# Second token layer of chunk pairs 0-1 and 3-4 as seven block products from batch 2 on

## The chip, the cores and the metric

One core of a Trainium2 chip runs the whole program. The metric is device time in microseconds (us), the median over several runs. The four runs of the kernel before agree within 0.1% (594.19 to 594.73 us); each run also reports the mean clock that TensorE was granted, as a share of full speed.

In this kernel TensorE does the matrix products into PSUM banks, ScalarE and VectorE move results out of these banks (an eviction) and add them up, and GpSimd does adds on SBUF, where the operands lie, and issues part of the transfers. In the views of the profile PE is TensorE, PEld its weight loads, DVE is VectorE, ACT ScalarE, POOL GpSimd and SP the queue of SyncE; `L913` is line 913 of the kernel, and `osb<-px` says that tile `osb` is written from `px`.

A wait is told here in one of two ways. The views count the idle time of TensorE after the recorded end of a product, and leave out what is under 0.15 us. That end is modelled: in the kernel before, a product of 512 columns is recorded with 0.379 us while the next starts after 0.215. So from start to start a wait is some 0.16 us longer than in the view; where a number below is counted so, the text says it.

## The reference, cut to what matters

```python
# x: (8, 3008, 256)
X = real(fft(fft(x, axis=1), axis=2))              # Fourier mixing
xt = X.transpose(0, 2, 1)
h  = maximum(xt @ w_tok1, 0) @ w_tok2              # token layers, 3008 -> 256 -> 3008
u  = X + h.transpose(0, 2, 1)
out = u + maximum(u @ w_ch1, 0) @ w_ch2            # channel layers, 256 -> 1536 -> 256
```

There are eight batches. The change concerns `@ w_tok2`, the second token layer, and the addition of X to it.

## The kernel before: the parts that matter

A batch's 3008 tokens are worked on in six chunks of 512 columns (`CW`). For each batch a generator yields the pieces of the Fourier and token layers; the main loop deals them out over 24 steps per batch, of some 2.9 us each, between the products of the channel layers of the batch before. The second token layer makes a chunk's two halves by two products each and one VectorE add:

```python
for c in range(NCH):
    if c in (1, 2):
        third(c)                     # 8 small products, ScalarE copy qs, two VectorE adds: yt
        yield
    ut = perb.tile([P, 2, CW], FP16, tag="ut", name="ut", bufs=4)
    # ... cuts: the last, shorter chunk; the first chunk of batch 0
    for h in range(2):
        pu = ps_f("pu")
        for th in range(2):
            nc.tensor.matmul(pu[:, 0:n], lhsT=uu[:, th, int(minus), h, :],
                             rhs=w2_cols(b, c)[:, th],
                             start=(th == 0), stop=(th == 1))
        # ... y: the part of yt that belongs to this half
        nc.vector.tensor_tensor(out=ut[:, h, 0:n]..., in0=pu[:, 0:n]..., in1=y..., op=AT.add)
    yield
```

The fold adds the mirrored half of the next input to the straight one. `xp` and `xm` come by transfers that GpSimd issues; the first add that reads `xm` waits for them:

```python
for s, (t0, t1) in enumerate(((13, 17), (9, 13), (5, 9), (1, 5))):
    # ...
    tt(out=xp[:, t, 1:D], in0=xp[:, t, 1:D], in1=xm[0:KR, rv, D - 1:0:-1], op=add)
    yield
    # ... then two or three adds into eo; yield between them
fold_plan = [[0] * 8 + [1, 2, 0, 0] * 4 for _ in range(BB)]     # pieces of it per step
```

The channel layers already use a seven-product scheme: VectorE makes `block_sums` of the activations `c1`, TensorE multiplies them into the banks `px` and `py`, and VectorE takes these banks out by `residual` into `osb`. The main loop, cut:

```python
for s in range(4):
    sub = 4 * c + s
    mm1(b, c, c1, range(3 * s, 3 * s + 3))    # first channel layer: pc -> c (ScalarE)
    # ... block_sums (VectorE), at once or after mm2, by s
    take(own, ...); take(nxt, ...)            # pieces of this batch and of the next
    mm2(*prev, s, pbox)                       # second channel layer: px, py -> osb
    take(nxt, ...)
    # ...
    take(folds, fold_plan[b][sub])            # fold of the batch after next
    if b and sub == 22 and b + 3 < BB:
        x_tiles[b + 3] = load_x(b + 3)        # GpSimd issues the loads of xp and xm
```

## Time and profile before

| | before |
|---|---|
| time, median of 4 runs | 594.2 us (594.19 to 594.73) |
| TensorE busy, matmuls | 580.4 us (98%), 6397 |
| VectorE busy | 458.7 us (77%) |
| ScalarE busy | 437.7 us (74%) |
| GpSimd busy | 152.7 us (26%) |

The prediction below shows the lines of the page, of the chain and of the waits. One more view is wanted for the comparison. I cut the trace at the first matmul of the first channel layer of each batch; these are batches 1, 2 and 3 before. The columns are: stretch in us, its length, then busy us and number of instructions of PE, weight loads, DVE, ACT and POOL, then the granted clock, the share of the DMA engines and GB/s.

```profile
100.52:170.22 69.70, 69.70 (x775) 50.30 (x774) 59.29 (x138) 52.55 (x122) 18.33 (x31) 1.00 0.50 93
170.22:240.89 70.67, 70.67 (x805) 51.45 (x804) 56.53 (x129) 52.88 (x122) 17.81 (x28) 1.00 0.47 91
240.89:310.53 69.64, 69.64 (x776) 50.28 (x775) 55.29 (x129) 52.53 (x122) 16.62 (x28) 1.00 0.48 91
```

TensorE's busy time equals the length of each batch. Odd and even batches differ by 1 us because of the chunk that two batches share, and the later batches repeat these two lengths.

### The profile page before, as it was taken

How to read it: one execution, taken by the hardware profiler on the slowest of the kernel's cores; microseconds unless marked ns; L12 is line 12 of the kernel's file. 1: busy time of each engine (PE TensorE's matmuls, PEld its weight loads, DVE VectorE, ACT ScalarE, POOL GpSimd, SP SyncE). 2: the span in 40 equal slices, each digit the busy share in tenths (PEclk: the TensorE clock that was granted, in tenths of full speed). 3: DMA queues.
4: the chain of work that ended last, by engine and by line, in shares of the span. 5: the costliest groups of instructions: out<-in, count | busy, mean ns of one | idle time of the engine just before them, and what ended most of it. 6: DMA issues, size and time to landing. Idle time of an engine off the chain costs nothing.

```text
span 592.4 us, 15959 instructions
## 1 busy us (share of the span) xinstructions
PE 580.4 (98%) x6397; PEld 419.8 (71%) x6397; DVE 458.7 (77%) x1075; ACT 437.7 (74%) x994; POOL 152.7 (26%) x251
## 2 busy tenths in 40 slices
PE   5999999999999999999999999999999999999997
PEld 4846777767776777676777667767777777866676
DVE  8868689878896887769797787868888677676573
ACT  7775887887778777777767776777777867766772
POOL 7530421412151211421134111421211121112131
PEclk9999999999999999999999999999999999999999
DMA  9996851863367242844329432492233335333424
GB/s 151 211 187 126 139 101 46 150 122 54 66 122 139 55 88 56 157 71 98 64 49 170 98 65 55 90 172 54 56 76 63 78 55 97 48 72 72 82 58 105
DMA packets 86683, 56.55 MB, mean 95 GB/s; under 512 B 54945, under 2 KB 83553, under 8 KB 85857
## 3 DMA queue, kind: packets, MB, share of 16 engines
q1 hardware_dynamic: 77984, 37.77, 33.6%
q0 software_dynamic: 8320, 17.49, 17.2%
q8 instruction: 50, 0.82, 0.6%
q10 hardware_dynamic: 304, 0.26, 0.2%
q14 instruction: 25, 0.20, 0.1%
HBM read 34.98 MB, written 24.64 MB: 101 GB/s over the span
## 4 chain that ended last, share of the span: by engine, by line
PE 96%; DVE 2%; ACT 1%; issue 0%; POOL 0%; DVEq 0%; POOLq 0%
PE pc L773 41%; PE px L817 25%; PE py L817 10%; PE pu L730 7%; PE pt L613 4%; PE po L888 2%; PE pz L518 2%; PE pq L645 1%; PE py L645 1%; PE py L836 1%; PE pw L596 1%; PE pw L597 1%; PE pw L560 0%; ACT z L307 0%; PE ph L430 0%; PE ph L432 0%
## 5 line engine op out<-in xcount | busy, mean ns | idle before, releaser
L776 ACT ACTIVATE c<-pc 128x512 f16<-128x512 f32 (+1 forms) x574 | 297.9, 595 | 31.3 <-PE pc L773 16.3
L799 POOL TENSOR_TENSOR osb<-osb,rt 128x256 f32<-128x256 f32 (+1 forms) x92 | 84.5, 919 | 373.3 <-DVE osb L799 366.1
L817 PEld LDWEIGHTS <-c 128*128 128x128 f16 x2112 | 128.1, 98 | 24.9
L773 PE MATMUL pc<-ut,wc1p 128*128 128x512 f16 x576 | 140.0, 379 | 0.5 <-DVE ut L305 0.5
L773 PE MATMUL pc<-ut,wc1m 128*128 128x512 f16 (+1 forms) x576 | 134.9, 370 | 0.0
L822 ACT ACTIVATE m<-px 128x256 f32<-128x256 f32 (+1 forms) x138 | 51.8, 375 | 75.4 <-PE px L817 46.0
L817 PEld LDWEIGHTS <-sb 128*128 128x128 f16 x1584 | 94.6, 98 | 10.4
L738 DVE TENSOR_TENSOR ut<-pu,yt 128x512 f16<-128x512 f32 (+1 forms) x94 | 63.3, 674 | 40.6 <-PE pu L730 40.3
L773 PEld LDWEIGHTS <-wc1p 128*128 128x128 f16 x576 | 52.0, 97 | 49.2 <-DMA wc1p<-in_moe_w_ch_dram,ixc 0.8
L773 PEld LDWEIGHTS <-wc1m 128*128 128x128 f16 x576 | 52.9, 98 | 45.0
L817 PE MATMUL px<-wst,c 128*128 128x128 f16 x1056 | 74.0, 219 | 0.0
L817 PE MATMUL px<-wc,c 128*128 128x128 f16 x1056 | 66.5, 219 | 0.0
L799 DVE TENSOR_TENSOR osb<-py,m 128x256 f32<-128x256 f32 (+1 forms) x92 | 37.5, 407 | 26.5 <-ACT m L822 26.2
L790 DVE TENSOR_TENSOR sb<-sb,c 128x768 f16<-128x768 f16 (+1 forms) x92 | 54.2, 589 | 3.2
L730 PE MATMUL pu<-w2p,uu 128*128 128x512 f16 (+1 forms) x184 | 54.7, 379 | 0.0
L790 DVE TENSOR_TENSOR sb<-c 128x768 f16<-128x768 f16 (+1 forms) x92 | 50.6, 550 | 0.0
L790 DVE TENSOR_TENSOR c<-c 128x768 f16<-128x768 f16 (+1 forms) x92 | 50.5, 548 | 0.0
L790 DVE TENSOR_TENSOR sb<-c,sb 128x768 f16<-128x768 f16 (+1 forms) x92 | 50.4, 548 | 0.0
L307 ACT ACTIVATE z<-pz 128x480 f16<-128x480 f32 (+1 forms) x60 | 39.0, 666 | 5.4 <-PE pz L527 3.0
L599 DVE SCALAR_TENSOR_TENSOR w<-alt,pw 128x131 f16<-128x131 f16 x84 | 29.2, 351 | 16.5 <-ACT w L307 16.0
L652 DVE TENSOR_TENSOR yt<-py,qs 128x512 f16<-128x512 f32 x48 | 30.9, 685 | 10.5 <-ACT qs L648 10.2
L817 PE MATMUL py<-wst,sb 128*128 128x128 f16 x528 | 37.1, 219 | 0.0
(201 smaller groups left out, 648.1 us busy)
## 6 DMA issues: line engine op xcount, KB each, us to landing
out_dram<-osb SPq DMA_DIRECT2D x83, 256.0 KB, 3.8
xp<-in_x_dram POOLq DMA_DIRECT2D x16, 272.0 KB, 5.3
out_dram<-osb SPq DMA_DIRECT2D x11, 192.0 KB, 3.1
xp<-in_x_dram POOLq DMA_DIRECT2D x16, 127.5 KB, 5.8
rt<-ut SPq DMA_TRANSPOSE x96, 3.8
w2s<-in_moe_w_tok_dram POOLq DMA_DIRECT2D x1, 1504.0 KB, 14.8
w1p<-in_moe_w_tok_dram POOLq DMA_DIRECT2D x4, 192.0 KB, 7.9
wc<-in_moe_w_ch_dram POOLq DMA_DIRECT2D x1, 768.0 KB, 15.2
```

Of the source, the lines that this page charges most:

```text
L307: nc.scalar.activation(out=out_, in_=in_, func=AFT.Copy)
L599: nc.vector.scalar_tensor_tensor(out=w[:, g, 0:131], in0=alt[:], scalar=pw[:, 131:132], in1=pw[:, 0:131], op0=AT.mult, op1=AT.add)
L613: nc.tensor.matmul(pt[:, o:o + n], lhsT=hw[:, g, th * P:th * P + P], rhs=w[:, g, f:f + n], start=(g == 0), stop=(g == NG - 1))
L652: nc.vector.tensor_tensor(out=yt[:, h, CW * c:CW * c + CW], in0=py[:], in1=qs[:], op=op)
L730: nc.tensor.matmul(pu[:, 0:n], lhsT=uu[:, th, int(minus), h, :], rhs=w2_cols(b, c)[:, th], start=(th == 0), stop=(th == 1))
L738: nc.vector.tensor_tensor(out=ut[:, h, 0:n].rearrange("p (a b) -> p a b", b=64), in0=pu[:, 0:n].rearrange("p (b a) -> p a b", b=64), in1=y ...
L773: nc.tensor.matmul(pc[:, 0:n], lhsT=wc[:, h, ct * P:(ct + 1) * P], rhs=ut[:, h, 0:n], start=(h == 0), stop=(h == 1))
L776: nc.scalar.activation(out=c1[:, ct, 0:n], in_=pc[:, 0:n], func=AFT.Relu)
L790: nc.vector.tensor_tensor(out=o, in0=x, in1=y, op=op)
L799: eng.tensor_tensor(out=o, in0=x, in1=y, op=AT.add)
L817: nc.tensor.matmul(o[:, t], lhsT=a(k)[:, f:f + P], rhs=w(k), start=(first and t == 0 and k == 0), stop=(k == HC - 1), skip_group_check=True)
L822: nc.scalar.activation(out=m[:, i, t1], in_=pa[:, 0], func=AFT.Copy)
```

## The change

Its intent is one product fewer in each 2x2 block of (two halves of the feature rows) x (two chunks), by sums of blocks: the weight sums are made once by GpSimd in batch 1, the sums of the activations for every batch by VectorE. The 7 products need 7 VectorE adds out of PSUM in place of 4, so the schedule of all pieces was laid out anew. The diff, cut to its core:

```diff
+    def w2_sums():                                  # once, in batch 1
+        for i, c in enumerate(PAIRS):               # PAIRS = (0, 3)
+            ...
+            for o, x, y in ((t1, b12, b11), (t2, b22, t1), (t3, b22, b12), (t4, b21, t2)):
+                pl.tensor_tensor(out=o, in0=x, in1=y, op=AT.subtract)
+                yield
@@ fold: mirror adds by themselves; from batch 4 on all four come first
+        if b >= 4:
+            for s, (t, rv) in enumerate(parts):
+                mirror(s, t, rv)
+                yield
@@ second token layer, from batch 2 on, chunks 0-1 and 3-4
+            mm(pa, uu[:, 0, m, 0, :], wa[:, 0], True)
+            plus(t0, pa, add_y(0, c), "v")
+            yield
+            mm(px, uu[:, 1, m, 0, :], wa[:, 1], True)
+            plus(into(ua, 0), px, t0)
+            yield
+            mm(pb, usum[:, 0, m, :], wsum[:, i, 0, :], True)
+            mm(pa, usum[:, 1, m, :], wsum[:, i, 1, :])      # adds to what is in pa
+            plus(t1, pa, add_y(0, c + 1), "v")
+            yield
+            ...                                             # pa, pa, pb again
@@ main loop
-    plan = [...] + [[1] * 14 + [2, 1] * 4 + [1, 1]] * (BB - 1)
+    plan = [...]                                    # pieces before and after mm2, by hand
+    sums_plan = [0, 1, 1, 2, 0, 0, 1, 1, 1, 0, 1, 0, 0, 0, 0, 0, 0, 0, 0, 0, 0, 0, 0, 0]
-    fold_plan = [[0] * 8 + [1, 2, 0, 0] * 4 for _ in range(BB)]
+    fold_plan = [[0, 1, 0, 0, 1, 0, 0, 0, 2, 1, 0, 0, 3, 0, 0, 0, 0, 2, 0, 0, 2, 0, 0, 0] for _ in range(BB)]
```

In the new `plan`, eight small products (`third`) and four second-layer products of chunk 2 are also done one batch earlier than before, so batch 1 has more to do and batch 7 less.

## The prediction

The forecast's sum for VectorE came to 31.7 us: the 36 adds of 0.686 us (24.7 us) and the activation sums. It came to 5.3 us in a middle batch with both pairs (60 to 63.6 of some 69.7 us, 86 to 91%) and to 3.2 us for the new pair in batch 1. The trace after shows 0.28 to 0.29 us for an activation sum, 6.9 us for the 24.

> **What bounds the kernel now.** I read the busy shares first, then the chain that ended last, then its pieces in order of time, then the waits of TensorE, then busy time by batch. The page:
>
> ```profile
> PE 580.4 (98%) x6397; PEld 419.8 (71%) x6397; DVE 458.7 (77%) x1075; ACT 437.7 (74%) x994; POOL 152.7 (26%) x251
> PE 96%; DVE 2%; ACT 1%; issue 0%; POOL 0%; DVEq 0%; POOLq 0%
> ```
>
> TensorE is busy 98% and the chain that sets the end is 96% TensorE. Busy alone would not settle it, since the recorded ends of matmuls are modelled. The chain's pieces between 229 and 238 us (start, length, what) do:
>
> ```profile
> 229.65 1.14 PE pc L773 x6
> 230.78 0.43 PE pu L730 x2
> 231.22 1.34 PE px L817 x24
> 232.56 0.43 PE pu L730 x2
> 232.99 1.13 PE pc L773 x6
> 234.12 0.67 PE py L817 x12
> 234.79 0.67 PE px L817 x12
> ```
>
> Each piece starts where the one before ends: 230.78 + 0.43 = 231.21, 231.22 + 1.34 = 232.56. There is no hole, and a second-layer product (the `pu` rows, 512 columns) occupies the chain for 0.43 / 2 = 0.215 us, not for the 0.379 us that its own row gives as duration. The waits of TensorE (engine, line waited for: us, times, longest) over the whole span:
>
> ```profile
> PE filler L294 <- DVE altu L325: 5.9, 1, 5.9
> PE pz L518 <- ACT tt L287: 0.6, 1, 0.6
> PE pc L773 <- DVE ut L305: 0.5, 1, 0.5
> ```
>
> Asked for the time after 40 us alone, this view lists no wait of TensorE. Busy time in two middle batches (stretch: us, PE, weight load, DVE, ACT, POOL):
>
> ```profile
> 110.30:181.10 70.80, 70.80 (x802) 51.30 (x801) 58.25 (x131) 53.13 (x124) 21.05 (x33) 1.00 0.58 106
> 181.10:250.60 69.50, 69.50 (x782) 50.38 (x779) 54.68 (x129) 51.83 (x122) 17.16 (x27) 1.00 0.46 89
> ```
>
> So a batch lasts as long as its matmuls need, at clock 1.00, and the other engines have room: VectorE 54.7 to 58.3 of some 70 us, GpSimd 17 to 21. Only less TensorE work can shorten it; other engines matter once they make TensorE wait. The rows for pricing (busy, mean ns of one, idle before it):
>
> ```profile
> L730 PE MATMUL pu<-w2p,uu 128*128 128x512 f16 x152 | 45.2, 379 | 0.0
> L738 DVE TENSOR_TENSOR ut<-pu,yt 128x512 f16<-128x512 f32 x78 | 53.4, 686 | 35.8 <-PE pu L730 35.6
> L790 DVE TENSOR_TENSOR sb<-c x92: 344/548/1523, 48.9 to 575.0; 128x768 f16<-128x768 f16 x84, 128x384 f16<-128x384 f16 x8
> L703 DVE COPY ut<-tail x4: 184/1184/1186, 135.4 to 554.2; 128x128 f16<-128x128 f16 x4
> ```
>
> The adds behind the second layer spend 35.8 us waiting for TensorE: VectorE is usually ahead.
>
> [...]
>
> **The change part by part.**
>
> TensorE: for chunk pairs 0-1 and 3-4 the 2x2 block product (two halves of the feature rows, two chunks) takes 7 products in place of 8. From batch 2 on that is 6 batches x 2 pairs x 1 = 12 matmuls of 512 columns fewer; the built program confirms it, with 24 rows fewer on TensorE (12 loads, 12 matmuls). All else on TensorE stays in kind and number. 12 x 0.215 = 2.6 us off the path, 0.43 us per batch. The loads lay under matmuls and count nothing. The columns are now contiguous for the summed blocks, which I price at nothing[...].
>
> VectorE: each pair had 4 adds from PSUM and now has 7 (three keep a running partial in SBUF, four finish a chunk half): 12 x 3 = 36 more x 0.686 = 24.7 us. The activation sums are 4 per batch of 128x256 in 16 bit. [...] Together 31.7 us: busy 458.7 becomes about 490, 83% of the span. [...] All of it lies beside TensorE as long as VectorE keeps up.
>
> GpSimd: 8 weight sums of 128x512, once, in batch 1. Its 128x512 residual add takes 1.17 us in the timeline, so I estimate 8 x 1.17 = 9.4 us: 21 becomes 30 of 70.8 us. [...] batch 1 has 70.8 - 58.3 = 12.5 us of VectorE slack and takes only the new pair 0-1[...].
>
> ScalarE: nothing added or removed. The order of `py` and `pq` is exchanged so that the bank which ScalarE reads is filled first; no cost.
>
> What moves: the interleaving of the pieces is laid out anew, and fold work goes earlier. The order of instructions shows the new dependences. The bank `pa` is written four times per pair with an add reading it in between, where each chunk half had its own bank before. Mostly a step of some 2.9 us (24 to a batch) lies between two writes. In the pair 0-1 from batch 2 on, the third and fourth write share a step with 24 small matmuls between them, 1.34 us. The need is 0.379 (first product's latency) + 0.686 (the add) = 1.07 us; from start to start there is 0.215 + 1.34 = 1.56 us. About 0.5 us is left, if VectorE is free at once.
>
> Sum: -2.6 us of matmuls, + new stalls. I choose 0.1 us per batch for six batches (a late VectorE now and then) and 0.1 us for GpSimd in batch 1: +0.7. 594.2 - 2.6 + 0.7 = 592.3 us, a gain of 0.3%.
>
> **The rivals.**
>
> 1. VectorE takes the matmul's place: at near 90% in a batch and strictly in order, it reaches the adds from `pa` late, and TensorE waits at the fourth write and at the block sums of the channel layer. For it: waits already make 12 to 15 us of idle VectorE time per batch, so useful room is less than the share suggests; the margin is only 0.5 us at one place. Against: most of these waits are for TensorE's own products, and the tight place comes once per batch. One stall of 0.4 us per pair would be 12 x 0.4 = 4.8 us: 594.2 - 2.6 + 4.8 = 596.4 us.
>
> 2. GpSimd holds VectorE up in batch 1. For it: the copy of `tail` took 1184 ns in place of 184. Against: it is one batch, there is slack. At worst some 2 us of stalls: about 593.6 us.
>
> 3. Nothing waits, and the re-laid schedule also clears what little TensorE loses in the middle: 591.6 us. Much below that isn't possible, for the matmuls left are the same and start and end of the program are as before.
>
> 4. The saved time is hidden anyway, because the end is set by the last batch's output. Against: the last batch also saves, its chain is TensorE to the end, and the tail after it is unchanged. It would give 594.2 us.
>
> **Range and chances.** The gain is bounded by 2.6 us; I give the full gain without new stalls a quarter, a gain of 1 to 2.4 us half, rival 1 or 2 in strength a quarter. With 0.5 us for the spread of runs (594.19 to 594.73 before), 8 in 10 lie between 591.2 and 594.6. Faster by over 2% would need 11.9 us, more than four times the removed work: 0.01. Slower by over 2% would need a stall of 14.5 us, 1.2 us in each of the 12 pairs: 0.02. The rest, 0.97, is within 2%.
>
> **What would show each step.** Right: 6385 matmuls, the chain still 96% TensorE without holes, batches of about 70.4 and 69.1 us, VectorE near 490 us busy, ScalarE within 1 us of before, GpSimd near 162, no TensorE wait after 40 us. New waits of TensorE for the VectorE rows that read `pa`, or for `sb` and `c`, would show rival 1; long block sums in batch 1 beside GpSimd's weight sums, rival 2. The prediction is wrong if the batches do not get shorter by about 0.4 us each, or if products on summed blocks run at another rate than 0.215 us.

## The result, and the profile after

The changed kernel takes 602.92 us (601.81 to 605.44, four runs) against 594.22. All outputs are right. A ratio here is the mean time of one kernel's runs over that of the other's in the same rounds, so it is not quite the ratio of the medians: 1.0147, 95% interval 1.0121 to 1.0173. It is within 2%, but slower, 8.7 us where 1.9 us of gain were predicted, and outside the range.

The page after, with the clock in fortieths of the span and the chain that ended last:

```profile
PE 582.8 (97%) x6385; PEld 419.6 (70%) x6385; DVE 487.3 (81%) x1135; ACT 438.8 (73%) x994; POOL 167.0 (28%) x259
...
PEclk9999999989999999999999999999999999999999
...
PE 14%; DVE 0%; issue 0%
```

The 12 matmuls are gone and the busy times are close to the predicted ones. But one slice of the clock has an 8, and the chain can be followed back only over the last 14% of the span: it broke at 516.8 us, behind a wait in batch 6, and says nothing of what came before. Shares and chain would have told little; the cut by batches tells more. Batches 1, 2 and 3 after:

```profile
101.74:178.05 76.31, 73.32 (x786) 51.75 (x785) 68.35 (x149) 53.03 (x123) 28.88 (x38) 0.98 0.43 83
178.05:251.61 73.56, 70.85 (x803) 51.33 (x802) 59.32 (x138) 53.06 (x122) 21.04 (x31) 1.00 0.52 96
251.61:321.78 70.17, 69.72 (x774) 50.18 (x772) 59.05 (x138) 52.74 (x122) 17.17 (x28) 1.00 0.47 90
```

Batch 1 grew from 69.70 to 76.31 us. Its 11 more matmuls are the 12 that moved there (8 of 128 columns, 4 of 512) less one of the first pair of batch 2; by start-to-start times of 0.056 and 0.215 us that is 8 x 0.056 + 3 x 0.215 = 1.1 us. The other 5.5 us are waits and a lowered clock. Batch 2 has two matmuls fewer (803 for 805) and is 2.9 us longer. Batches 3 to 6 are 1.5 us longer together, though each lost 0.43 us of products. Batch 7 is shorter, mostly by what moved out of it. The waits of TensorE after the first 38 us (line waited for: us in all, times, longest), of which the kernel before had none after 40 us:

```profile
PE px L931 <- DVE osb L913: 3.2, 6, 1.9
PE py L931 <- DVE osb L913: 2.3, 1, 2.3
PE px L931 <- DVE c L904: 0.4, 1, 0.4
PE pc L887 <- ACT c L890: 0.4, 2, 0.2
PE pa L751 <- DVE tc L760: 0.3, 1, 0.3
```

Of 6.8 us in the view (a sixth line, of 0.2 us, is cut) 5.5 are for `osb`, the eviction of the channel layers' banks by VectorE: not for the adds of the new product. Only 0.3 us is a wait for a read of `pa`. Counted from start to start, and with the slower clock of which more below, TensorE lost 5.7 us in batch 1, 3.4 in batch 2 and 3.5 in batches 3 to 6. Two waits of some 2 us stand out.

**The wait in batch 1.** VectorE, GpSimd and TensorE around 117 us, from the timeline (start, length, what, idle before and who ended it):

```profile
116.57 0.63 DVE L904 TENSOR_TENSOR sb<-c 128x768 f16<-128x768 f16 x1
117.24 3.22 DVE L904 TENSOR_TENSOR sb<-sb,c 128x768 f16<-128x768 f16 x1
120.38 0.41 DVE L913 TENSOR_TENSOR osb<-px,m 128x256 f32<-128x256 f32 x1
```

```profile
116.72 1.01 POOL L913 TENSOR_TENSOR osb<-osb,rt 128x256 f32<-128x256 f32 x1
117.70 1.19 POOL L469 TENSOR_TENSOR w2s<-w2p 128x512 f16<-128x512 f16 x1
118.85 1.19 POOL L469 TENSOR_TENSOR w2s<-w2p,w2s 128x512 f16<-128x512 f16 x1
```

```profile
120.84 0.33 PE L931 MATMUL px<-wst,sb 128*128 128x128 f16 x3 [1.95 <-DVE osb L913]
```

An add of two SBUF operands that takes 0.56 us at the median took 3.22. It ends 0.4 us after the third of three GpSimd instructions that followed one another without a gap (116.72 to 120.04 us; a small copy of 0.52 us comes next): it seems to have got no turn between them, which is my reading of these times. The eviction behind it came late, and TensorE waited 1.95 us. What followed is in the granted clock, the third number from the right in these stretches of the same kernel:

```profile
118.00:120.80 2.80, 0.90 (x14) 0.71 (x12) 2.80 (x3) 1.17 (x3) 2.51 (x3) 1.00 1.02 173
120.80:122.00 1.20, 1.16 (x23) 1.15 (x23) 1.20 (x2) 0.29 (x2) 1.13 (x2) 1.00 0.97 167
122.00:125.60 3.60, 3.60 (x17) 1.68 (x14) 0.59 (x2) 2.70 (x6) 1.25 (x1) 0.55 1.21 212
125.60:130.00 4.40, 4.40 (x50) 3.07 (x48) 3.64 (x9) 3.24 (x8) 0.14 (x1) 0.98 0.00 0
```

From 122.00 to 125.60 us TensorE ran at 0.55 of its clock in the mean, a loss of 0.45 x 3.6 = 1.6 us more. TensorE counts as fully busy in it, so no view of waits shows this loss.

**The wait in batch 2.**

```profile
190.19 0.23 DVE L483 TENSOR_TENSOR xp<-xp,xm 94x16 f16<-94x16 f16 x1 [6.40 <-DMA xm<-in_x_dram,ix]
190.30 0.68 DVE L484 TENSOR_TENSOR xp<-xp,xm 94x1020 f16<-94x1020 f16 x1
190.90 0.41 DVE L913 TENSOR_TENSOR osb<-py,m 128x256 f32<-128x256 f32 x1
```

VectorE stood idle for 6.4 us until a load of the input had landed. The new fold plan has the first mirror add in step 1 of the batch (counted from 0), where it was in step 8; the load is still issued at the change of batch, which is at 178.05 us: GpSimd issues `xp` from 176.81 us and `xm` at 179.23 and 180.51. The eviction of `py` was in the queue behind the fold, and TensorE waited 2.34 us for it.

So there are four suspects: the sums on GpSimd, the early fold, the lowered clock, and small waits in the later batches. A rival to all of them is that seven products cost TensorE as much as eight.

### The profile page after: what moved, and what is told of

The parts are those of the page before. It is cut to its first block, busy times and chain, and to the rows that moved or that the text cites. A ratio compares the mean times of both kernels' runs of the same rounds, so it can differ in the third digit from the quotient of the medians.

```text
span 603.6 us, 15998 instructions
## 1 busy us (share of the span) xinstructions
PE 582.8 (97%) x6385; PEld 419.6 (70%) x6385; DVE 487.3 (81%) x1135; ACT 438.8 (73%) x994; POOL 167.0 (28%) x259
## 5 line engine op out<-in xcount | busy, mean ns | idle before, releaser
L913 POOL TENSOR_TENSOR osb<-osb,rt 128x256 f32<-128x256 f32 (+1 forms) x92 | 85.9, 934 | 381.9 <-DVE osb L913 369.5
L913 DVE TENSOR_TENSOR osb<-py,m 128x256 f32<-128x256 f32 (+1 forms) x92 | 37.4, 407 | 34.2 <-ACT m L936 33.8
L904 DVE TENSOR_TENSOR sb<-c 128x768 f16<-128x768 f16 (+1 forms) x92 | 56.0, 608 | 0.0
L904 DVE TENSOR_TENSOR sb<-c,sb 128x768 f16<-128x768 f16 (+1 forms) x92 | 51.9, 564 | 0.0
L904 DVE TENSOR_TENSOR c<-c 128x768 f16<-128x768 f16 (+1 forms) x92 | 50.5, 548 | 0.0
L931 PE MATMUL px<-wst,sb 128*128 128x128 f16 x528 | 37.0, 219 | 3.2 <-DVE osb L913 3.2
L931 PE MATMUL py<-wc,sb 128*128 128x128 f16 x528 | 37.0, 219 | 2.3 <-DVE osb L913 2.3
L314 ACT ACTIVATE z<-pz 128x480 f16<-128x480 f32 (+1 forms) x60 | 37.2, 726 | 2.6 <-PE pz L561 1.7
L852 DVE TENSOR_TENSOR ut<-pu,yt 128x512 f16<-128x512 f32 (+1 forms) x46 | 29.9, 658 | 8.8 <-PE pu L849 8.6
```

The lines of the kernel that those rows point to most:

```text
L314: nc.scalar.activation(out=out_, in_=in_, func=AFT.Copy)
L852: nc.vector.tensor_tensor(out=ut[:, h, 0:n].rearrange("p (a b) -> p a b", b=64), in0=pu[:, 0:n].rearrange("p (b a) -> p a b", b=64), in1=a ...
L904: nc.vector.tensor_tensor(out=o, in0=x, in1=y, op=op)
L913: eng.tensor_tensor(out=o, in0=x, in1=y, op=AT.add)
L931: nc.tensor.matmul(o[:, t], lhsT=a(k)[:, f:f + P], rhs=w(k), start=(first and t == 0 and k == 0), stop=(k == HC - 1), skip_group_check=True)
```

## The experiments

### Each suspect alone, put into the kernel before

Only the eight weight sums, which nothing reads:

```diff
+    sums_plan = [0, 1, 1, 2, 0, 0, 1, 1, 1, 0, 1] + [0] * 13
+    w2_parts = w2_sums()
...
+                if b == 1:
+                    take(w2_parts, sums_plan[sub])
```

Theory A is the hold read above, 3.22 us for an add of 0.56.

> The kernel before plus nothing but the eight weight sums on GpSimd in batch 1, in the steps where the changed kernel has them; their results are not used. Theory A ([...]TensorE waits over 2 us at one place in batch 1 and then runs some 3.5 us at about half clock): the time rises by 2 to 5 us over the kernel before, all of it in batch 1, with one block sum of VectorE over 2.5 us long. Rival (the sums are harmless, batch 1 of the changed kernel is longer because its new interleaving overloads VectorE): within 0.5 us of before.

Measured: 596.12 us, ratio 1.0032 (1.0016 to 1.0049). Batch 1 is 71.56 us in place of 69.70, and TensorE has two waits that were not there:

```profile
PE py L832 <- DVE osb L814: 0.7, 1, 0.7
PE px L832 <- DVE c L805: 0.7, 1, 0.7
```

The clock stayed full. The sums cost 1.9 us by themselves, a little less than expected, in a batch in which VectorE is less loaded than in the changed kernel (59 us busy in the kernel before, 68 in the changed one). The expected long block sum is there: `c<-c` at 117.78 us took 3.40 us (the 92 of this kind take 54.6 us in all, 50.5 in the kernel before), beside four GpSimd instructions in a row (117.66 to 120.77), two of them weight sums, and ended 0.4 us after the last, as in the changed kernel. The expected wait of over 2 us is not: behind this sum stood another sum, and TensorE lost 0.7 us. So here, with 3.40 us of hold for 0.7 us of wait, it was not the length of the hold alone that counted, but what stood behind it.

Only the new fold and its plan:

```diff
-    fold_plan = [[0] * 8 + [1, 2, 0, 0] * 4 for _ in range(BB)]
+    fold_plan = [[0, 1, 0, 0, 1, 0, 0, 0, 2, 1, 0, 0, 3, 0, 0, 0, 0, 2, 0, 0, 2, 0, 0, 0] for _ in range(BB)]
```

> The kernel before with nothing but the changed kernel's fold order and fold plan, whose first mirror add stands in step 1 of a batch in place of step 9. Theory B (the first mirror add waits at the head of VectorE's queue for the load of x of that batch, which was issued only three steps earlier): VectorE waits 4 to 8 us for the landing of xm in batch 2, TensorE loses about 2.5 us there, and the time rises by 2 to 3.5 us over before; later batches lose under 0.5 us each. Rival (batch 2's loss comes from batch 1's delay or from the block products): no wait of VectorE for xm over 1 us, time within 0.7 us of before.

Measured: 595.81 us, ratio 1.0027 (1.0010 to 1.0043). Batch 2 is 72.35 us in place of 70.67, with one wait:

```profile
PE py L828 <- DVE osb L810: 1.4, 1, 1.4
```

VectorE stood idle for 3.73 us before the first mirror add of batch 2. Both suspects are real, and each was smaller here than expected. In the changed kernel they are larger. That the same batches also hold the new adds there would explain it; this is argued and not shown. The runs with parts taken out, below, show that the two suspects also act on each other.

### Each suspect taken out of the changed kernel

The sums on VectorE in place of GpSimd:

```diff
-                pl.tensor_tensor(out=o, in0=x, in1=y, op=AT.subtract)
+                nc.vector.tensor_tensor(out=o, in0=x, in1=y, op=AT.subtract)
```

> The changed kernel with the eight weight sums on VectorE in the same steps. Theory A: no VectorE instruction in batch 1 is longer than 1.5 us, no stretch of lowered clock after 40 us; the time falls by 3 to 5.5 us below the changed kernel's (602.9), to 597.5 to 600. Rival (VectorE's load itself makes batch 1 long): VectorE has 4 us more to do there, and the time stays or rises above 603.

Measured: 599.43 us (598.40 to 599.65), ratio 1.0089. Batch 1 fell from 76.31 to 72.17 us and no stretch of lowered clock is left. A sum takes 0.42 us on VectorE; on GpSimd it took 1.19 to 1.51. Giving VectorE, the fuller engine, 3.3 us more work made the kernel 3.5 us faster, as expected: what the sums cost on GpSimd was the hold that they had on VectorE, up to the 3.22 us of one add. The fold stood where it was, yet TensorE's wait in batch 2 fell from 2.34 to 0.64 us and that batch to 71.94 us.

The sums spread, one at most in a step:

```diff
-    sums_plan = [0, 1, 1, 2, 0, 0, 1, 1, 1, 0, 1, 0, 0, 0, 0, 0, 0, 0, 0, 0, 0, 0, 0, 0]
+    sums_plan = [0, 0, 0, 0, 0, 1, 1, 0, 0, 1, 1, 0, 0, 1, 1, 0, 0, 0, 1, 0, 0, 0, 1, 0]
```

> The changed kernel with the eight weight sums still on GpSimd but spread: at most one to a step, in steps 5, 6, 9, 10, 13, 14, 18 and 22 of batch 1, away from GpSimd's residual adds and from the load of x. Theory A (back-to-back GpSimd instructions lock VectorE out): no VectorE instruction in batch 1 over 1.8 us, no TensorE stall over 1 us there, no lowered clock; time 598 to 600 (changed kernel 602.9, sums on VectorE 599.4). Rival (any GpSimd work of this size costs the same wherever it stands): above 601.5.

Measured: 601.49 us, ratio 1.0128; the four runs are 599.17 and 600.08 at clocks 0.999 and 1.0, 602.90 and 603.01 at 0.997 and 0.996. The two runs at full clock are what was expected, the median is not. Batch 1 took 73.42 us in the profile. Spreading shortens the worst wait of batch 1, from 2.1 us to 1.0 (start to start), but several remain. Batch 2 fell too, from 73.56 to 71.44 us, though nothing in it was changed. In the profiled run, a fast one, nothing waited longer than that; what lowered the clock in the other two runs was not seen.

The first two mirror adds of batch 2 in steps 5 and 6:

```diff
+    fold_plan[2] = [0, 0, 0, 0, 0, 1, 1, 0, 2, 1, 0, 0, 3, 0, 0, 0, 0, 2, 0, 0, 2, 0, 0, 0]
```

> The changed kernel with the first two mirror adds of batch 2 moved from steps 1 and 4 to steps 5 and 6, all else the same. Theory B: the wait of VectorE for xm in batch 2 shrinks from 6.4 us to under 1, TensorE's stall of 2.5 us at that place goes, and the time falls by 2 to 3 us, to 600 to 601. Rival (VectorE's total load in batch 2 sets its length): under 0.7 us.

Measured: 601.81 us, ratio 1.0132. Batch 2 fell from 73.56 to 71.45 us, so beside the bunched sums the early fold was worth 2.1 us of it. The four runs fall apart again: 599.86 and 600.60 at clock 1.0, which is what was expected, 603.34 and 603.03 at 0.996. The profile fell on a run at full clock: it has the same wait of 1.9 us in batch 1, and no lowered clock after it. So the wait does not always bring the lowered clock with it, and the runs with a lower mean clock are some 2.9 us longer.

Both at once:

> The changed kernel with the sums spread and the first mirror adds of batch 2 moved to steps 5 and 6. If theories A and B are separate terms their gains add: 596.8 to 598.5. Rival (one hides the other): no better than the better of the two alone, about 599.

Measured: 598.81 us (598.63 to 599.44), ratio 1.0077. That is 0.3 us above the range in which the two gains simply add, and close to the 599 of the rival. The runs no longer fall apart. The batches say how far the two are one term: batches 1 and 2 together took 149.87 us in the changed kernel, 5.0 less with the sums spread, 3.8 less with the fold late, and only 5.5 less with both. Once the sums are spread, moving the fold takes batch 2 from 71.44 to 70.99 us, 0.45 and not 2.1. One reason can be read: from the second issue of `xm` to the add that waits for it there were 9.7 us in the changed kernel and 7.5 with the sums spread. Why the load took longer is not shown. With the two large waits gone, 4.6 us above the kernel before are left.

### The small waits

I moved `third` behind the channel product of its step, one of the writes of `pa` to another place, and one `z` piece to a neighbouring step, and made the first mirror adds late in all batches:

```diff
-    plan += [list(zip([0, 0, 1, 0, 0, 0, 0, 0, 1, 0, 0, 1, 0, 2, 0, 0, 1, 2, 1, 0, 1, 0, 0, 0],
-                      [2, 1, 2, 2, 0, 1, 0, 1, 2, 1, 1, 2, 2, 0, 0, 2, 0, 0, 0, 0, 1, 1, 2, 1]))] * (BB - 2)
+    plan += [list(zip([0, 0, 0, 0, 0, 0, 0, 0, 1, 0, 0, 1, 0, 2, 0, 0, 0, 2, 1, 0, 1, 0, 0, 0],
+                      [2, 2, 2, 2, 0, 1, 0, 1, 2, 1, 1, 2, 2, 0, 0, 2, 1, 0, 0, 0, 1, 1, 2, 1]))] * (BB - 2)
```

(and the same in batch 1's lists)

> As x6_both, and three pieces moved within the interleaving: the middle third of the first-layer products of the token inverse (pq, py) behind the channel product of its step in place of before it, one write of pa in batch 1 behind that product as well, one z piece out of the step that held three; late first mirror adds for all batches. Theory C (the repeating stalls of 0.4 us at px and 0.36 or 0.18 us at pc and px in batches 2 to 6 come from VectorE's and ScalarE's queues at two crowded steps, not from the number of instructions): these stalls go, each of batches 3 to 6 gets shorter than the same batch of the kernel before by 0.3 to 0.45 us, time 593 to 595.5. Rival (VectorE is simply too full with 31 us more): the stalls move elsewhere, time stays at 597 or so.

Measured: 596.88 us (596.79 to 597.50), ratio 1.0045 (1.0029 to 1.0062). A wait of 0.41 us (start to start) for `osb`, which every batch from 2 to 6 had behind the two adds of `third`, is gone. The time is above the expected 595.5 all the same: batch 1 is still 73.27 us, and TensorE still loses 0.2 to 0.8 us in each of batches 2 to 6. By the time alone the rival, a VectorE that is simply too full, did as well (597 or so); the later plans, with the same work in another order, speak against it.

### Is the saved product worth anything?

To the kernel of the last run I added the eighth product back, by issuing the second product of each pair twice. It writes the same values again:

```diff
-            mm(px, uu[:, 1, m, 0, :], wa[:, 1], True)
+            for _ in range(2):
+                mm(px, uu[:, 1, m, 0, :], wa[:, 1], True)
```

> As x7_relaid, with the second product of each pair issued twice (the second overwrites the first with the same values): 8 products per pair in place of 7, 12 matmuls of 512 columns more, nothing else. If TensorE's chain sets the time, it takes 12 x 0.215 = 2.6 us more than x7_relaid (2.2 to 2.8). Rival (VectorE or the waits set the time and matmuls are hidden): under 1 us more.

Measured: 598.60 us against 596.88. In the traces each step with the doubled product is 0.21 to 0.22 us longer, and the last product of the first channel layer comes 2.41 us later. One of the twelve fell into a wait and cost nothing. The rival is dead: in this kernel a removed product is worth its 0.215 us where TensorE does not wait. Of the 2.4 us, 1.7 were seen in the time; in the two profiles the rest lay in how long the last transfers took after the last product.

### What a wait does to the clock

The runs that fell apart by clock left a question open: is it the wait of 2 us that lowers the clock, or something else in that stretch? I put waits of my own into the kernel before, by useless additions on VectorE in one step of batches 1 to 6:

```diff
+    dm = const.tile([P, 384], FP32, name="dm")
+    nc.vector.memset(dm[:], 0.0)
...
+                if 1 <= b <= 6 and sub == 8:
+                    for _ in range(8):
+                        nc.vector.tensor_tensor(out=dm[:], in0=dm[:], in1=dm[:], op=AT.max)
```

> The kernel before, with eight useless VectorE additions (128x384, fp32[...]) in the ninth step of batches 1 to 6. VectorE has some 1 us to spare there, so TensorE should wait some 1.5 to 2.5 us, six times: 594.2 + 9 to 15 us = 603 to 609 us if a wait costs only itself. If a wait of this length lowers TensorE's clock afterwards, the runs add 2 to 3 us for each wait that does it: the granted clock then falls to 0.99 in such runs, the times of the runs spread by several us, and the profile shows stretches near half clock right after these waits.

and with twelve in place of eight (the length of all twelve is cut in the same way; 613 to 618 us rest on it):

> The same with twelve additions[...], a wait of 3 to 4 us six times: 613 to 618 us if a wait costs only itself. If waits lower the clock and longer ones do it more surely, most or all of the six waits are followed by a stretch of lowered clock here, 2 to 3 us more each, some 628 us, with a mean clock of 0.98; if the clock has another cause it stays at 0.997 to 1.0 as in the kernel before.

Measured: 625.41 us with eight (624.33 to 626.13), 643.11 with twelve. An addition took 0.56 us, longer than expected, so the waits were longer than meant, 3.3 us in the mean (3.6 at most) and 5.6 us (6.0 at most), and both times lie above the expected ones. The waits alone explain this much of the first:

```profile
PE px L819 <- DVE c L792: 19.5, 6, 3.6
```

The kernel is 31.1 us slower, so 11.6 us are not waits, 1.9 us for each of the six. With twelve additions it is 48.9 us less 33.8 us of waits, 2.5 us each. The profile of the first shows what these are (around the wait in batch 2, then around that in batch 3):

```profile
205.70:209.40 3.70, 0.26 (x4) 0.08 (x2) 3.59 (x9) 0.84 (x2) 0.00 (x0) 0.86 0.02 4
209.40:210.60 1.20, 1.07 (x11) 1.07 (x12) 1.20 (x5) 0.00 (x0) 0.00 (x0) 0.50 0.00 0
210.60:214.00 3.40, 3.40 (x17) 1.75 (x16) 2.93 (x7) 2.26 (x5) 0.00 (x0) 0.50 0.00 0
...
285.60:286.80 1.20, 1.15 (x14) 0.92 (x15) 1.20 (x4) 0.44 (x2) 0.00 (x0) 1.00 0.00 0
286.80:290.00 3.20, 3.20 (x22) 2.24 (x21) 3.01 (x8) 1.90 (x4) 0.00 (x0) 0.51 0.00 0
```

In both, TensorE works at half clock after the wait (0.50 and 0.51); where it starts, within the wait or 1.2 us after it, differs. All twelve waits of the two profiles are followed by such a stretch: windows of 2.5 to 3.5 us after each show a clock of 0.50 to 0.54. In these windows GpSimd is idle and the DMA engines are nearly so (0.00 to 0.03), which rules these out as its cause here. So each of these waits cost itself plus 1.9 us in the mean with eight additions, and plus 2.5 us with twelve.

Why does a shorter wait do it in some runs only? The kept traces go further than the stretches above, for they hold the times at which the granted clock changed. In the changed kernel it falls from 1.00 to 0.50 at 122.33 us and is back at 1.00 after 3.41 us. With eight additions the falls come at 133.29, 208.38, 286.89, 361.98, 437.07 and 512.17 us, which lie 22, 23, 22, 22 and 22 times 3.413 us apart (378.88 us in all, 111 times 3.4133). I laid out two stretches of that length around each large wait of the changed kernel, counted from its fall at 122.33 us (columns as before):

```profile
118.91:122.33 3.42, 1.49 (x24) 1.29 (x24) 3.29 (x4) 0.88 (x3) 3.06 (x4) 1.00 1.03 174
122.33:125.74 3.41, 3.41 (x15) 1.68 (x14) 0.53 (x1) 2.37 (x5) 0.92 (x1) 0.50 1.18 204
187.18:190.59 3.41, 1.74 (x17) 1.00 (x15) 0.40 (x2) 3.39 (x8) 0.00 (x0) 1.00 1.66 180
190.59:194.01 3.42, 2.64 (x27) 1.69 (x27) 3.39 (x9) 1.71 (x4) 0.00 (x0) 1.00 0.65 124
```

The wait of 1.95 us lies in one stretch, which is idle for 1.93 us, and the next stretch runs at half clock. The wait of 2.34 us is the longer one, but it lies across two: 1.67 and 0.78 us are idle in them, and the clock stays full. So the length of a wait alone did not decide here. That its place among such stretches does would fit the two groups of runs, but it was my estimate from these two waits; no run tests it, and the slower runs of these kernels have no profile in which to see it. The stretch of 3.41 us at half clock costs 1.7 us; what else such a run loses of its 2.9 us is not seen.

### Is there a version that beats both?

Six more kernels dealt VectorE's work out anew, starting from the one at 596.88 us. The first two were to take at most two fold adds or one weight sum beside the block sums of a step (the list has one step with three pieces of the fold all the same), with five sums in batch 1 and three in batch 2, or all eight in batch 1 (the lists of pieces, re-dealt as well, are cut):

```diff
+    sums_plan = {1: [0, 0, 0, 0, 0, 1, 1, 1, 1, 0, 1, 0, 0, 0, 0, 0, 0, 0, 0, 0, 0, 0, 0, 0],
+                 2: [0, 1, 1, 1, 0, 0, 0, 0, 0, 0, 0, 0, 0, 0, 0, 0, 0, 0, 0, 0, 0, 0, 0, 0]}
+    fold_plan = [[0, 0, 0, 0, 0, 1, 2, 0, 1, 0, 0, 0, 2, 0, 3, 0, 0, 0, 1, 0, 2, 0, 0, 0] for _ in range(BB)]
+    fold_plan[1] = [3, 3, 0, 0, 0, 0, 0, 0, 0, 2, 2, 2, 1, 1, 1, 1, 0, 0, 0, 0, 2, 0, 0, 0]
```

> The re-laid kernel with its VectorE and ScalarE work dealt out by the load of each step: at most two fold adds or one weight sum beside the block sums, mirror adds from the sixth step of a batch on, five weight sums in batch 1 and three in the first steps of batch 2. If the remaining stalls (some 2.5 us in batch 1, 0.4 to 0.6 us in each of batches 2 to 6) come from VectorE and ScalarE work that is bunched within a step, most go: batch 1 some 71.5 us, batches 2 to 6 some 0.3 us shorter each, 593 to 595.5 us in all. If they come from GpSimd holding VectorE up whatever the step, batch 1 stays at 73 us, and the time near 596.5.

> As the run before it, but all eight weight sums stay in batch 1, at most one in a step. If bunching is the cause, 593 to 595.5 us, and within 0.5 us of the run before it. If each sum costs its 0.2 to 0.3 us wherever it lies, batch 1 is longer here by some 0.7 us and batch 2 shorter by the same, and the two kernels take the same time; if batch 2 takes its three sums for nothing, the run before it is 0.7 us faster.

Measured: 598.69 and 600.65 us, both misses. Batch 1 was as hoped in the first (71.84 us), so the sums do cost less when three of them are in batch 2; but batches 2 to 5 got a new wait of 0.98 us each (start to start) for `osb`, soon after the step with two fold adds. The load of a step, added up from its instructions, was not the measure; the place in the queue was. The next two only moved fold adds:

```diff
-    fold_plan = [[0, 0, 0, 0, 0, 1, 2, 0, 1, 0, 0, 0, 2, 0, 3, 0, 0, 0, 1, 0, 2, 0, 0, 0] for _ in range(BB)]
+    fold_plan = [[0, 0, 0, 0, 0, 1, 1, 0, 1, 1, 1, 0, 3, 0, 0, 0, 0, 2, 0, 0, 2, 0, 0, 0] for _ in range(BB)]
```

> As the kernel with eight sums dealt over batches 1 and 2 (598.7 us), but with one fold step fewer in the step before the one in which its batches 2 to 6 lost 0.98 us, and without the three fold steps at once that led to 0.2 us. If those stalls come from the fold steps standing ahead of the output's eviction in VectorE's queue, 0.2 to 0.3 us is left of the 0.98 in each of five batches: batches 2 to 6 at 70.0 to 70.9 us, 594 to 596 us in all. If VectorE is short of time whatever the order, the stall only moves to another step, and the time stays near 598.

```diff
+    fold_plan = [[0, 0, 0, 0, 0, 1, 0, 0, 2, 1, 1, 0, 3, 0, 0, 0, 0, 2, 0, 0, 2, 0, 0, 0] for _ in range(BB)]
+    fold_plan[1] = [3, 3, 0, 0, 0, 0, 0, 0, 0, 2, 2, 1, 1, 0, 1, 1, 0, 0, 2, 0, 1, 0, 1, 0]
```

> As the run before it, with no fold step at all in the two steps before the one that stalled, and in batch 1 the fold steps drawn from its fifteenth step towards its end. If the order within VectorE's queue is the cause, no stall over 0.1 us is left in the eighth step of batches 2 to 6 and batch 1 falls from 71.8 to some 71 us: 593 to 594.5 us, so at least level with the kernel before (594.2). If not, it stays within 0.5 us of the run before it.

Measured: 595.81 us (ratio 1.0021), then 594.47 us (594.28 to 595.50), ratio 1.0005, interval 0.9988 to 1.0022. That is level with the kernel before. Both times are as expected, though batch 1 stayed at 71.68 us where some 71 was. The wait of 0.98 us shrank to 0.38 and then vanished, as the theory of the queue's order has it. The seven-product batches of the last one (batches 1, 2 and 3):

```profile
100.52:172.20 71.68, 71.22 (x787) 51.03 (x786) 64.50 (x147) 52.77 (x123) 24.46 (x32) 1.00 0.46 88
172.20:243.11 70.91, 70.54 (x803) 51.30 (x802) 60.59 (x140) 52.88 (x122) 25.75 (x36) 1.00 0.54 99
243.11:312.47 69.36, 69.36 (x774) 50.12 (x773) 59.27 (x138) 52.52 (x122) 17.50 (x27) 1.00 0.52 91
```

Batch 3 is now 0.28 us shorter than before (69.64), but batch 1 still carries waits. Two last tries moved the fold adds of batch 1, later and earlier:

```diff
+    fold_plan[1] = [3, 3, 0, 0, 0, 0, 0, 0, 0, 2, 2, 0, 0, 2, 1, 1, 1, 0, 2, 1, 0, 0, 0, 0]   # later
+    fold_plan[1] = [3, 3, 0, 0, 0, 0, 0, 0, 2, 1, 2, 1, 1, 0, 1, 1, 0, 1, 0, 0, 2, 0, 0, 0]   # earlier
```

(the second also splits the three fold steps at once of batches 2 to 6)

> The level kernel (594.47) with the fold steps of batch 1 moved off the three places that still stall, 0.41, 0.37 and 0.54 us. If the time follows the order within VectorE's queue there too, batch 1 falls from 71.7 to some 71 us and batch 2 from 70.9 to 70.5: 593.2 to 593.9 us, a little below the kernel before. If the stalls move elsewhere, 594.5 or more.

> The level kernel (594.47) with the fold steps of batch 1 that stood in its steps 18 and 22 moved to its ninth step, and the three at once of batches 2 to 6 split. Batch 1 stalled 0.41, 0.37 and 0.54 us there, and batches 2 to 5 0.14 us each. If the place in VectorE's queue decides, 0.9 us of the first and 0.5 us of the second go: 593.0 to 593.7 us. If VectorE is full in batch 1, the wait comes back in another step: 594.2 to 595.5.

Measured: 595.52 us (ratio 1.0015) and 595.92 us (1.0034). Both are misses: batch 1 went to 73.17 and 73.38 us, and the waits came back elsewhere, as one of 1.2 and one of 0.9 us in the first and one of 1.7 us for `c` in the second (start to start). Batch 1, in which the sums, the fold of two batches and the first new pair meet, has no free place that these plans found.

## Why the prediction was wrong

**Right.** 6385 matmuls; 0.215 us for a removed product, shown by putting it back, 2.41 us for eleven (the products on summed blocks follow one another after 0.216 us as well); VectorE at 487 us (predicted 490), ScalarE at 438.8 against 437.7, GpSimd at 167 (162). The saving itself was sized right: 2.41 us to the last product of the first channel layer, where 2.6 were predicted and one product of twelve fell into a wait.

**Wrong: the term "+ new stalls", 0.7 us.** Between the two profiles the waits and the lowered clock are, after taking out the moved and the removed products: 5.5 us in batch 1; 2.9 + 0.43 = 3.3 us in batch 2; 1.5 + 4 x 0.43 = 3.2 us in batches 3 to 6. That is some 12 us in place of 0.7. The profiled run was the slowest of the four (605.44 us) and also began 1.2 us late behind a weight load; at the median it is some 8.7 + 2.6 = 11 us. The step that failed is the sentence that 31.7 us of new VectorE work lie "beside TensorE as long as VectorE keeps up". It was judged by the share of a batch (86 to 91%), while the test is, step by step, whether an eviction of `px` or `py` has an instruction ahead of it. That it was the order and not the amount is shown by the best of the later plans: with the same 6385 products and 1135 VectorE instructions it takes 594.47 us, 8.4 us less than the changed kernel.

**Rival 2, GpSimd in batch 1: right kind, wrong size.** "At worst some 2 us" was measured as 1.9 us in the kernel before, where I had drawn the slack from, and as 4.1 us in the changed kernel (76.31 to 72.17 with the sums on VectorE). The sums were priced as their own length; what they did was to hold one VectorE add through three GpSimd instructions (3.22 us in place of 0.56), ahead of an eviction. The slack was also misread. Batch 1 was said to take "only the new pair 0-1", 3.2 us for VectorE; it also took the four adds of the pieces moved there, and its VectorE went from 59.29 to 68.35 us, 9.1 us more, of which 4.4 are longer block sums (28.06 us for 23.65, 47 in each). And the 12.5 us of slack came from a stretch that starts 10 us into the batch; the batch itself has 69.70 - 59.29 = 10.4.

**Rival 1, the re-writes of `pa`:** 0.3 us of waits in all. I had looked for the new stall at the new product, and it was at the old one.

**Not named at all: the fold.** "Fold work goes earlier" was written down and priced at nothing. It made VectorE wait 6.4 us for a load whose issue had not moved, and that cost 2.1 us of batch 2 (what undoing it there gave back), 1.6 us when it was put into the kernel before by itself, or 0.45 us beside spread sums.

**Not named at all: the clock.** After the 1.95 us wait TensorE lost a further 1.6 us by its clock in the profiled run. That a wait is enough is shown by the runs with waits put in, of 3.3 and 5.6 us in the mean. Of the three waits of about 2 us in the profiles, two left the clock full: that of 2.34 us, and that of 1.9 us in the run with the late fold. Why is not shown, and not settled is what lowered the clock in the two slower runs with spread sums.

**The rest of the time.** Taking the sums apart and the fold late gave 598.8, the places of `third` and `z` 596.9, the remaining order of the queue 594.5. That last kernel keeps some 1.5 us of waits in batch 1 and at the start of batch 2, so an estimate from its trace for a plan without any is 593 us. No run reached it, and whether any plan does stays open.

## What to carry to other kernels

Where one engine is the bound without a hole, price added work on another engine by what stands behind it in that engine's queue, not by the share of time that is free; a piece moved earlier can also wait for a load that was not moved (6.4 us here). A wait on TensorE can cost time again by the clock (here 1.6 us after one of 1.95 us, nothing after one of 2.34, some 2 us after each of those of 3.3 and 5.6 us in the mean), which no list of waits shows, so look at the granted clock by stretches, and at whether runs fall into two groups. And lay out a re-timed schedule with the one-time work, here eight sums, away from the batch that is already the fullest.
